# Another order of issue for the pieces of a long-convolution and top-8 expert block

## The chip, the cores and the metric

The kernel runs on one core of one Trainium2 chip. The metric is the device time of one execution in microseconds (us). The engines that compute are TensorE (PE; its weight loads are shown as PEld), VectorE (DVE), ScalarE (ACT) and GpSimd (POOL). SyncE (SP) issues most of the transfers (DMAs); GpSimd and ScalarE issue some. Each engine works through its own queue in the order in which the program issued to it, and waits for others by semaphores.

## The reference, cut to what matters

2048 tokens of width D = 640, bf16. Two residual steps, both with a modulation from one condition vector `c`:

```python
mod = silu(c) @ w_mod                 # 6 rows of 640: sa, ca, ga, sb, cb, gb
h = layernorm(x) * (1 + ca) + sa
kv = short_conv4(k, shift_k) * v      # causal, 4 taps per channel
y = irfft(rfft(pad(kv)) * rfft(pad(ssm_k)))[:2048] + kv * ssm_D
x = x + ga * (h * y)
h = layernorm(x) * (1 + cb) + sb
r = h @ w_r; idx = top 8 tokens of r
y = (silu(h[idx] @ w_gate) * (h[idx] @ w_up)) @ w_down * sigmoid(r[idx])
out = x + gb * (h + scatter_add(y at idx))
```

## The kernel before, in words

The channels are cut into five blocks b = 0 to 4 of 128. For each block the long convolution of 4096 points is done as a two-stage Fourier transform by matmuls, on the kernel rows (`u = 0`, from `gA`) and on the data (`u = 1`, from `xA`). The work is cut into small pieces, each a Python generator step, and a list written out by hand, `ORDER` (lines 35 to 46), says in which order the pieces are issued. `run` (line 886) takes one step of the named task for each entry; `:n` takes n steps, and a star sets `evac.vector`, so that the piece is evacuated from PSUM by VectorE and not by ScalarE (in the C and AT pieces a star means a copy by ScalarE and then a multiply by VectorE, and no star one multiply by VectorE straight from PSUM). The list has 325 steps. Below, BT1.3 means the fourth step (counted from 0) of task BT1, and a position is the place of a step in the list, from 0 to 324. Nothing is reordered later: a piece's instructions go to the end of each engine's queue when it is issued. Buffers come from rings by tag, so an allocation waits until an older tile of its tag is no longer read.

The pieces, with their lines:

- SA to SH, SB, SC, SD, SE, SG, RA, RAT, TAB, WU, TC: constants, sine tables, a warm-up of TensorE (199 to 326). SG loads the diagonal `Dt` (240). IT (328) transposes the tables `FT` into `IT`.
- LG, LK, LXA, LX, LW, LU, WG, WD: loads. LG loads `gA` (140). LK clears 16 columns of `kT` on GpSimd (128) and loads `kT`, `vT` with transposing DMAs (129, 130). LXA loads `xA` from the scratch `kvd` (145). LX loads a quarter of `xq` (643). LW.a loads column block a of `w_mod` into one of two halves of `early` (553), and needs MOD.(a-2) done. LU loads `uA` from the scratch `Ud` (438). WG loads five pieces of the gate weights and five of the up weights (676, 682), WD two pieces of the down weights, issued by ScalarE (688, 690, 691).
- DIAG builds the four diagonal matrices of the short convolution on GpSimd (309); C does the convolution on TensorE, multiplies by `vT` and stores `kvd` (367 to 373).
- G and X: first stage for `gA` (after an addition of `Dt` on GpSimd, for block 0 on VectorE, 353) and `xA`, four pieces each into `A` (346). BG and BX: second stage, four pieces each into `HX` (386 to 390). P: complex product on VectorE, in place (406 to 410). BT: first inverse stage (422, 424), into `U`, stored to `Ud` by GpSimd (428; by SyncE for block 4). AT: last inverse stage with `uA` (457), times `h`; AA adds it into `xq` (468).
- MOD.a: modulation row a (565), evacuated by ScalarE (569, 571); OG, GB and COL combine the rows. Sx: statistics of the first layer norm on VectorE (649), with the power on GpSimd at the end (652). H: `h` in twelve steps (660, 664, 666); `h` lies in the memory of `early`, so H.0 waits for MOD.5.
- R transposes `xq` for the second norm and for r (523, 533), GR forms the squared sums (478). T.0 to T.9: second norm's scale, top 8, the expert, the scatter into the output. BS, BL prepare the base of the output (TensorE with the identity, 498, 499, or VectorE, 493), N normalizes (709, 712), F multiplies, adds and stores the output (720 to 723).

PSUM tiles rotate through four places, so a piece on TensorE also waits for the evacuation of the piece four before it.

Of the kernel before, what the change touches and what calls it, by code (L numbers as in the profile page):

```python
# [32 lines left out]


ORDER = """
SC SA RA WU LG0 SB0 TAB0 SD SG TAB0 SE LG1 LK0 SB1 RA G0 TAB1 G0*:2 G0 DIAG0 G1 SH LX G1* TAB1 LK1 DIAG1 RAT G1*
BG0* C0:2 IT Sx:2 IT* IT Sx LX LXA0 BG0 C1 G1 C1 BG1:2 Sx LG2 LXA1 Sx BG1 RAT BG0* X0:3 X0* Sx:2 BG1 TC BG0
DIAG3 BX0* BX0:2 DIAG2 LK2 X1 Sx P0 X1 LW LX P0 BX0 G2 C2:2 MOD X1 P0 X1* Sx LW Sx G2 LW BT0 G2 BX1* BX1:3 LXA2
P0 G2 MOD LX P1 LK3 Sx BT0 LG3 P1 Sx BT0 Sx BT0 LW Sx X2 Sx X2 MOD X2 BG2 Sx X2 OG Sx C3*:2 BX2 BG2 BT1 BG2 G3
P1 BX2 BG2 G3* MOD G3 BX2 P2 G3 DIAG4 LW BX2 BT1 LXA3 MOD P1 BT1 LW X3 LK4 X3 P2 BT2 MOD X3 LG4 P2:2 BT2 H:4 BT1  # L40
C4* X3 H BG3:2 C4 G4 BX3 LXA4 BX3 G4 LU1 G4 H G4 BG3 H P3 BX3 BG3* LU0 BX3 BT2 P3 X4 H X4 P3 X4 WG X4 H:2 BT2
BG4 WG:2 BG4 BX4* BX4:2 BG4:2 BX4 P3 LU2 P4 BT3 P4 BT3:3 P4 BT4 P4 H COL BT4:3 H GB AT0* COL AT0* LU3 AA0:2
AT1*:2 AA1:2 AT2* LU4 AT2* R0 WG AA2 AT3* R1 R0 GR WG:2 AA2 WG AT3 AA3:2 AT4* WG R1 R2 AT4 AA4 R3 GR AA4 R2 BS*
WD GR R4 BS* R3 BS* GR:2 WD GR R4 BS T BS WG BL N T N:4 N* N BS N:2 F T F N F N:2 F:2 T F:2 N BS WG BL N T N F T
F N F:2 BS F:4 T F T:3
"""


# [908 lines left out]
```

## Time and profile before

| | |
|---|---|
| time, median of 3 runs | 181.32 us (180.77 to 181.73) |
| the profiled execution | 181.52 us, its span 179.7 us |
| busy: PE, DVE, ACT, POOL | 150.0, 145.2, 138.3, 38.4 us |
| TensorE clock granted, mean | 0.899 of full speed |
| moved by DMA | 40.71 MB |

Times in the profile are counted from the first instruction. PE's busy time overlaps from matmul to matmul, since they are pipelined; the next start tells more than an end. In brackets stands how long the engine was idle ahead of an instruction, and who released it; "issue" means that the profile shows nothing that it waited for.

### The profile page before, as it was taken

The page shows a single profiled execution, that of the slowest core. Times are in us where ns is not written, and L with a number is a line of the kernel's source. Part 1 is how long each engine was busy: PE and PEld are TensorE (multiplying, and loading weights), DVE is VectorE, ACT ScalarE, POOL GpSimd, SP SyncE. Part 2 cuts the span into 40 slices and gives each one's busy share as a digit, 9 for nine tenths or more (in the row PEclk, how much of TensorE's full clock was granted, in tenths as well). Part 3 has the DMA queues.
Part 4 walks back from the last instruction along what each step waited for, and adds up shares of the span by engine and source line. Part 5 has one row for each costly group of instructions (what it writes and reads, how often), then busy time and mean ns, then how long its engine had stood idle before and what let it go on. Part 6 is the DMA issues. An engine that isn't in the chain of part 4 may idle for free.

```text
span 179.7 us, 4741 instructions
## 1 busy us (share of the span) xinstructions
PE 150.0 (83%) x1987; PEld 117.8 (66%) x1987; DVE 145.2 (81%) x265; ACT 138.3 (77%) x149; POOL 38.4 (21%) x86
## 2 busy tenths in 40 slices
PE   2879999994999999999999899996699549277850
PEld 0255868861698769886689699896699423137640
DVE  7199997989499938998999999997669537897940
ACT  3979759993499999999989999976849207999500
POOL 8529942000001168210500010200001002200003
PEclk9999999999699999999999999999569957967555
DMA  6799989999799996999939993794993994045640
GB/s 117 89 225 280 253 232 280 159 244 371 225 284 268 295 298 211 283 236 277 313 151 220 295 363 121 205 405 171 303 344 63 336 326 105 21 175 146 218 150 2
DMA packets 71437, 40.71 MB, mean 227 GB/s; under 512 B 45112, under 2 KB 68216, under 8 KB 71416
## 3 DMA queue, kind: packets, MB, share of 16 engines
q1 hardware_dynamic: 66440, 33.99, 73.5%
q0 software_dynamic: 1232, 4.21, 6.3%
q10 hardware_dynamic: 3744, 2.22, 4.3%
q8 instruction: 15, 0.25, 0.6%
q14 instruction: 6, 0.05, 0.1%
HBM read 24.67 MB, written 10.50 MB: 196 GB/s over the span
## 4 chain that ended last, share of the span: by engine, by line
PE 40%; DVE 21%; DMA 18%; POOL 6%; issue 5%; SPq 4%; ACT 4%; POOLq 1%; DVEq 0%; ACTq 0%
DMA kT<-in_A_k_dram 5%; PE ps L457 5%; PE ps L386 4%; DMA early<-in_w_mod_dram 4%; DVE st L649 4%; DMA Dt<-in_A_ssm_D_dram 3%; PE p L367 3%; PE ps L367 3%; SPq L129 3%; PE ps L523 3%; POOL dg L309 3%; DMA uA<-Ud 2%; DVE A L58 2%; PE ps L390 2%; PE ps L388 2%
## 5 line engine op out<-in xcount | busy, mean ns | idle before, releaser
L386 PE MATMUL ps<-A,FT 128*128 128x256 bf16 x132 | 30.2, 273 | 0.0
L60 ACT CAST HX<-ps 128x1024 bf16<-128x1024 f32 x28 | 28.3, 1078 | 2.2 <-PE ps L390 2.2
L390 PE MATMUL ps<-A,FT 128*128 128x128 bf16 x132 | 29.0, 219 | 0.0
L388 PE MATMUL ps<-A,FT 128*128 128x128 bf16 x132 | 28.9, 219 | 0.0
L60 ACT CAST A<-ps 128x1024 bf16<-128x1024 f32 x26 | 26.2, 1051 | 2.5 <-PE ps L346 2.4
L390 PEld LDWEIGHTS <-FT 128*128 128x128 bf16 x160 | 15.6, 98 | 1.8
L428 POOL DMA_DIRECT2D Ud<-U x8 | 4.7, 593 | 54.1 <-ACT U L60 54.1
L388 PEld LDWEIGHTS <-FT 128*128 128x128 bf16 x160 | 15.6, 98 | 0.7 <-issue 0.2
L386 PEld LDWEIGHTS <-FT 128*128 128x128 bf16 x160 | 15.6, 98 | 0.4
L60 ACT CAST U<-ps 128x1024 bf16<-128x1024 f32 x15 | 15.7, 1129 | 0.1
L422 PE MATMUL ps<-IT,HX 128*128 128x256 bf16 x60 | 13.7, 273 | 0.0
L424 PE MATMUL ps<-IT,HX 128*128 128x256 bf16 x60 | 13.7, 273 | 0.0
L649 DVE BATCH_NORM_STATS2 st<-xq 128x6 f32<-128x320 bf16 x32 | 13.3, 478 | 0.0
L367 PEld LDWEIGHTS <-dg 128*128 128x128 bf16 x80 | 7.6, 98 | 8.5 <-issue 0.6
L309 POOL TENSOR_SCALAR dg<-ident,shk_f 128x128 bf16<-128x128 bf16 x16 | 11.7, 748 | 4.2 <-PE ps L367 2.5
L407 DVE TENSOR_TENSOR HX<-HX 128x2048 bf16<-128x2048 bf16 x10 | 12.2, 1225 | 0.3
L60 ACT CAST base<-ps 128x1024 bf16<-128x1024 f32 x7 | 6.8, 1007 | 7.0 <-PE ps L499 7.0
L406 DVE TENSOR_TENSOR T<-HX 128x2048 bf16<-128x2048 bf16 x10 | 12.2, 1217 | 0.0
L457 PEld LDWEIGHTS <-uA 128*128 128x128 bf16 x160 | 10.4, 107 | 2.4 <-DMA uA<-Ud 2.2
L457 PE MATMUL ps<-RAT,uA 128*128 128x128 bf16 x128 | 9.4, 240 | 2.0 <-DMA uA<-Ud 2.0
L565 PE MATMUL ps<-early 128*128 128x320 bf16 x50 | 8.9, 333 | 2.6 <-DMA early<-in_w_mod_dram 2.6
L346 PEld LDWEIGHTS <-gA 128*128 128x128 bf16 x80 | 7.4, 98 | 4.4 <-DVE gA L353 2.0
(257 smaller groups left out, 395.2 us busy)
## 6 DMA issues: line engine op xcount, KB each, us to landing
uA<-Ud SPq DMA_DIRECT2D x10, 512.0 KB, 6.5
early<-in_w_mod_dram SPq DMA_DIRECT2D x6, 800.0 KB, 6.3
Ud<-U POOLq DMA_DIRECT2D x8, 512.0 KB, 5.2
gA<-in_A_ssm_k_dram SPq DMA_DIRECT2D x5, 512.0 KB, 5.0
xq<-in_A_q_dram SPq DMA_DIRECT2D x4, 640.0 KB, 5.7
kvd<-kvT SPq DMA_DIRECT2D x10, 256.0 KB, 3.0
xA<-kvd SPq DMA_DIRECT2D x5, 512.0 KB, 5.4
wg<-in_B_w_gate_dram SPq DMA_DIRECT2D x5, 432.0 KB, 7.2
```

Source lines behind the costliest of these rows:

```text
L60: self.nc.scalar.copy(out=out, in_=in_)
L309: (V if b == 0 else nc.gpsimd).tensor_scalar(out=dg[:, j, :], in0=ident[:], scalar1=shk_f[:, b, j:j + 1], scalar2=None, op0=ALU.mult)
L367: nc.tensor.matmul(ps[:, i, :], lhsT=diags[b][:, j, :], rhs=kT[:, n0 - j:n0 - j + 512], start=(j == 0), stop=(j == 3))
L386: nc.tensor.matmul(ps[:, i], lhsT=FT[:, 0, k2, :], rhs=A[:, 2 * k2:2 * k2 + 2, u, :], start=True, stop=False)
L388: nc.tensor.matmul(ps[:, i, 0, :], lhsT=FT[:, 1, k2, :], rhs=A[:, 2 * k2 + 1, u, :], start=False, stop=False)
L390: nc.tensor.matmul(ps[:, i, 1, :], lhsT=FT[:, 2, k2, :], rhs=A[:, 2 * k2, u, :], start=False, stop=True)
L406: V.tensor_tensor(out=T2[:], in0=X, in1=Hi, op=ALU.mult)
L407: V.tensor_tensor(out=X, in0=X, in1=Hr, op=ALU.mult)
L422: nc.tensor.matmul(ps[:, i, :], lhsT=hx[:, k2, 0, 1, :], rhs=IT[:, k2, 1:3, :].rearrange("p a b -> p (a b)"), start=True, stop=False)
L424: nc.tensor.matmul(ps[:, i, :], lhsT=hx[:, k2, 1, 1, :], rhs=IT[:, k2, 0:2, :].rearrange("p a b -> p (a b)"), start=False, stop=True)
L457: nc.tensor.matmul(o, lhsT=uA[:, bb, cs * P:(cs + 1) * P], rhs=RAT[:, cs, :].rearrange("p (m e) -> p m e", e=8), start=(cs == 0), stop=(cs ...
L649: V.bn_stats(out=st1[:, m, hf, :], in_=xq[:, m, hf * 320:hf * 320 + 320])
```

## The change

`ORDER` is replaced; no other line differs. The same 325 steps are issued, each once. 25 of them change their star.

```diff
@@ -33,16 +33,16 @@
 
 
 ORDER = """
-SC SA RA WU LG0 SB0 TAB0 SD SG TAB0 SE LG1 LK0 SB1 RA G0 TAB1 G0*:2 G0 DIAG0 G1 SH LX G1* TAB1 LK1 DIAG1 RAT G1*
-BG0* C0:2 IT Sx:2 IT* IT Sx LX LXA0 BG0 C1 G1 C1 BG1:2 Sx LG2 LXA1 Sx BG1 RAT BG0* X0:3 X0* Sx:2 BG1 TC BG0
-DIAG3 BX0* BX0:2 DIAG2 LK2 X1 Sx P0 X1 LW LX P0 BX0 G2 C2:2 MOD X1 P0 X1* Sx LW Sx G2 LW BT0 G2 BX1* BX1:3 LXA2
-P0 G2 MOD LX P1 LK3 Sx BT0 LG3 P1 Sx BT0 Sx BT0 LW Sx X2 Sx X2 MOD X2 BG2 Sx X2 OG Sx C3*:2 BX2 BG2 BT1 BG2 G3
-P1 BX2 BG2 G3* MOD G3 BX2 P2 G3 DIAG4 LW BX2 BT1 LXA3 MOD P1 BT1 LW X3 LK4 X3 P2 BT2 MOD X3 LG4 P2:2 BT2 H:4 BT1
-C4* X3 H BG3:2 C4 G4 BX3 LXA4 BX3 G4 LU1 G4 H G4 BG3 H P3 BX3 BG3* LU0 BX3 BT2 P3 X4 H X4 P3 X4 WG X4 H:2 BT2
-BG4 WG:2 BG4 BX4* BX4:2 BG4:2 BX4 P3 LU2 P4 BT3 P4 BT3:3 P4 BT4 P4 H COL BT4:3 H GB AT0* COL AT0* LU3 AA0:2
-AT1*:2 AA1:2 AT2* LU4 AT2* R0 WG AA2 AT3* R1 R0 GR WG:2 AA2 WG AT3 AA3:2 AT4* WG R1 R2 AT4 AA4 R3 GR AA4 R2 BS*
-WD GR R4 BS* R3 BS* GR:2 WD GR R4 BS T BS WG BL N T N:4 N* N BS N:2 F T F N F N:2 F:2 T F:2 N BS WG BL N T N F T
-F N F:2 BS F:4 T F T:3
+LG1 SC SB0 SA SD TAB0 SG SB1 LG0 WU LK0 SE RA:2 TAB0 TAB1 SH RAT G1:2 DIAG0 G0*:2 LX TAB1 DIAG1 G0* IT* LK1 RAT
+C0*:2 LX G0 G1* Sx IT G1* BG0 IT* LXA0 C1:2 BG0 BG1* LG2 LXA1 LK2 LW BG1 Sx BG0 Sx X0 Sx:2 BG1 X0 X0* LX X0 Sx
+BG0 BG1 BX0* BX0 BX0* DIAG2 TC P0 X1 BX0 P0 LW X1 G2 C2 X1 C2 MOD Sx X1 LW Sx LXA2 P0 LX G2 Sx G2 BT0 DIAG3 P0
+BX1* LK3 BX1:2 MOD LG3 G2 BX1 P1:2 BT0 Sx BT0:2 Sx BG2 MOD X2:2 Sx X2 Sx:4 BT1 X2 Sx BG2 LW C3 C3* P1 BX2:2 BG2
+BX2 G3* P2 G3 LW BX2 DIAG4 BG2 P1 OG G3 LXA3 MOD LW P2 G3 MOD BT1:2 P2 X3 BT1 BG3* LK4 X3 P2 LG4 MOD H WG H X3
+BG3 BT2 H X3 H C4*:2 H BX3 WG BX3:3 P3 BT2 H BT2 H BG3 BG3* G4:2 BT2 G4:2 LXA4 X4 P3 LU1 H X4:2 LU0 H X4 BG4:2
+BT3 P3 H BX4* P3 BX4:3 BG4 P4 WG BG4 BT3 P4 BT3 LU2 BT3 P4 WG BT4 P4 H BT4 COL H BT4:2 AT0* AT1 AA0 AT0* LU3 AA1
+AA0 AT2* AT1* AT2* AA1 AA2:2 R0 COL AT3 GB R1 AA3 R0 LU4 WG:2 GR AT3* AA3 AT4* R2 R1 WG AA4 GR AT4 R3 GR AA4 BS*
+R2 R4 WD R3 BS* GR:2 WG BS* WG GR R4 T BL N* BS N:5 T F T N F:2 WG N WD F:2 BS N BS N T N F:2 BS BL T F:2 N F
+N:2 F:2 N F T F N BS F T F T:3
 """
 
 
```

Positions of steps that the text below speaks of, before and after:

| step | before | after | step | before | after |
|---|---|---|---|---|---|
| LG0.0, LG1.0 | 4, 11 | 8, 0 | LK4.0 | 148 | 152 |
| TAB1.0, RAT.0 | 16, 28 | 15, 17 | BT1.3 | 162 | 150 |
| G0.0, G1.0 | 15, 21 | 21, 18 | C4.0, C4.1 | 163, 168 | 166, 167 |
| IT.0, C0.0 | 33, 31 | 27, 30 | G4.0, BX3.3 | 169, 184 | 181, 173 |
| C1.0, C1.1 | 42, 44 | 41, 42 | BT2.3 | 196 | 183 |
| LK2.0, LW.0, LX.2 | 68, 73, 74 | 47, 48, 59 | LXA4.0, X4.0 | 171, 187 | 186, 187 |
| MOD.0, X1.2 | 80, 81 | 79, 77 | WG.0, WG.1 | 192, 198 | 158, 170 |
| Sx.6, Sx.7, Sx.8 | 59, 70, 84 | 80, 83, 88 | WG.3 | 239 | 216 |
| Sx.16, OG.0 | 121, 120 | 120, 138 | BT3.0, BT3.3 | 210, 214 | 198, 214 |
| LW.4, MOD.4 | 139, 143 | 133, 145 | GB.0 | 224 | 241 |
| MOD.3, LW.5, MOD.5 | 133, 146, 152 | 141, 142, 156 | LU3.0, LU4.0 | 228, 236 | 229, 245 |
| H.0 | 158 | 157 | WD.0, R4.0, WD.1 | 263, 265, 271 | 264, 263, 291 |

Stars: to VectorE go G0.0, IT.0, IT.2, G1.3, BG1.0, X0.2, BX0.2, G3.0, BG3.0, N.0; from VectorE go G1.1, BG0.0, IT.1, BG0.2, X0.3, X1.3, G3.1, N.5; a copy by ScalarE is added to C0.0, C0.1, C4.1, AT3.1 and taken from C3.0, AT1.0, AT3.0.

## Rows read from the trace of the kernel before

**Rows 1.** Busy us by stretch: PE, PEld, DVE, ACT, POOL, clock, DMA share, GB/s.
```profile
44.40:117.40 73.00, 72.00 (x704) 59.39 (x705) 65.75 (x99) 68.25 (x76) 15.02 (x17) 0.98 0.95 254
```
**Rows 2.** Timeline of PE around the first modulation product: start, us, engine, line.
```profile
39.92 1.89 PE L367 MATMUL ps<-kT,dg 128*128 128x512 bf16 x8
44.43 2.83 PE L565 MATMUL ps<-early 128*128 128x320 bf16 x10 [2.62 <-DMA early<-in_w_mod_dram]
47.05 1.00 PE L346 MATMUL ps<-RA,xA 128*128 128x256 bf16 x4
47.89 0.60 PE L346 MATMUL p<-RA,xA 128*128 128x256 bf16 x4
```
**Rows 3.** The waits of VectorE: waited for, us in total, times, longest.
```profile
DVE gA L353 <- DMA Dt<-in_A_ssm_D_dram: 3.0, 1, 3.0
...
DVE A L58 <- PE p L346: 2.7, 2, 2.3
```
**Rows 4.** Timeline of SyncE's queue, three issues of loads.
```profile
37.66 0.57 SPq L553 DMA_DIRECT2D early<-in_w_mod_dram  x1
...
73.19 1.15 SPq L553 DMA_DIRECT2D early<-in_w_mod_dram  x1
74.52 5.60 SPq L129 DMA_TRANSPOSE kT<-in_A_k_dram  x1
```
**Rows 5.** Groups by line: an evacuation by VectorE: busy, mean ns.
```profile
L58 DVE CAST HX<-ps 128x1024 bf16<-128x1024 f32 x5 | 6.1, 1216 | 0.2 <-PE ps L390 0.2
```
**Rows 6.** Issue to landing by tile: early (w_mod), kT, xA.
```profile
DMA to landing us min/median/max: 5.1/6.3/9.7
...
DMA to landing us min/median/max: 5.8/7.5/9.9
...
DMA to landing us min/median/max: 4.3/5.4/7.3
```
**Rows 7.** Timeline of POOL: block 1's store, kT4's clear, block 3's store.
```profile
78.76 0.63 POOL L428 DMA_DIRECT2D Ud<-U  x1 [5.70 <-ACT U L60]
79.40 0.13 POOL L128 MEMSET kT<- 128x16 bf16 x1
...
115.21 0.53 POOL L428 DMA_DIRECT2D Ud<-U  x1 [1.29 <-ACT U L60]
```
**Rows 8.** Timeline of SyncE's queue: loads of uA, for block 2, then 3 and 4.
```profile
112.09 1.00 SPq L438 DMA_DIRECT2D uA<-Ud  x2
...
123.15 3.98 SPq L438 DMA_DIRECT2D uA<-Ud  x4
```
**Rows 9.** Timeline of VectorE: P4's last step, AA4's two steps.
```profile
114.94 0.68 DVE L410 TENSOR_TENSOR HX<-HX,T 128x1024 bf16<-128x1024 bf16 x1
...
137.79 1.28 DVE L468 TENSOR_TENSOR xq<-xq,t 128x1024 bf16<-128x1024 bf16 x2
```
**Rows 10.** Timeline of PE: AT3's first matmuls, then R4.0 to GR.4.
```profile
127.27 1.89 PE L457 MATMUL ps<-RAT,uA 128*128 128x128 bf16 x16 [2.04 <-DMA uA<-Ud]
...
139.13 1.01 PE L523 MATMUL ps<-ident,xq 128*128 128x128 bf16 x15
141.25 0.23 PE L523 MATMUL ps<-ident,xq 128*128 128x128 bf16 x1 [1.10 <-issue]
141.31 0.54 PE L533 MATMUL pq<-wcol,xT 128*128 128x3 bf16 x16
141.78 1.07 PE L478 MATMUL pg<-xT 128*32 128x32 bf16 x104
143.22 0.22 PE L478 MATMUL pg<-xT 128*32 128x32 bf16 x7 [0.37 <-ACT xT L527]
146.34 0.31 PE L478 MATMUL pg<-xT 128*32 128x32 bf16 x17 [2.90 <-issue]
```
**Rows 11.** Timeline of VectorE in the last part: T.1's first step, F.0.
```profile
151.56 0.28 DVE L753 CAST T<-pq 16x128 f32<-16x128 bf16 x1 [0.32 <-PE pq L751]
...
154.12 0.82 DVE L720 TENSOR_TENSOR FT<-FT,modv 128x1280 bf16<-128x1280 bf16 x1 [0.59 <-ACT FT L712]
```

## The prediction

> **What bounds the kernel now.** I read the long windows first, then the PE timeline, then the waits, and last each queue beside the two lists of pieces. Between 44.4 and 117.4 us PE is busy for 72.0 of 73.0 us, ACT for 68.3 and DVE for 65.8 [rows 1]: three engines are nearly full at once, so an order can win there only what is idle, a few us. The one large hole ahead of that stretch is the first modulation product: C2's last piece begins at 39.92 and is issued in 1.7 us, then PE stands for 2.62 us until w_mod's first column block lands, and the product runs at the half clock, 2.83 us [rows 2]. VectorE stood for 3.0 us at the start for Dt, and 2.7 us in all for evacuations of A behind that product [rows 3]. The tail is different: a chain of transfers, small VectorE steps and dense small matmuls, with holes of several us [rows 8 to 11]. So I look for the gain in the tail, and for the risk in the full stretch.
>
> **The loads that move but do not.** SyncE issues in list order, and it is compared with itself, not with the pieces between. Taken alone, its order is LG2, LXA1, LK2, LW.0, LX.2 before and after; LW.0 was issued right behind kT2 and vT2, at 37.66 [rows 4]. Moving LW.0 up 25 places and LK2 up 21 therefore moves neither. They still hang on kvd1, that is on C1. I cost them at 0.
>
> **The front (items 0 to 78).** Block 1's gA goes first and the tables of the second half and of RAT are put under the 3.0 us wait for Dt [rows 3]; that is up to 3.0 us of VectorE work hidden. Against it: G1's addition is on GpSimd, gA0's addition now stands behind these tables on VectorE, and IT.0 is issued ahead of C0 and needs the second table's cosines. The best case is 3.0 us earlier, the worst as much later as PE now stands at MOD.0, 2.6 us, without any loss. Since MOD.0 waits for a transfer whose place on SyncE is unchanged, I take 0.
>
> **MOD.0.** One piece, X1.2, passes ahead of it: 0.84 us of PE at the half clock (47.05 to the next piece at 47.89) [rows 2] moves into the hole. Sx.6, Sx.7 and Sx.8 fill VectorE there, in place of most of the 2.7 us it stood for A [rows 3]. I take -0.6; the ends are 0 and -2.2 (the product at the other level as well: 2.83 down to about 1.4).
>
> **The full stretch (items 79 to 224).** Nothing is added, but the marks change: nine evacuations go to VectorE and seven leave it, 1.22 us each [rows 5], so about +2.4 us there; of the C pieces three become a copy on ACT plus a multiply out of SBUF and one goes back, which returns a part. OG's two multiplies pass behind Sx.16. So VectorE has 1 to 2.5 us more to do in this stretch, and it is earlier by the 2 us won at MOD.0. New waits: MOD.3 is 8 places later, so LW.5, which needs its buffer, is issued later than 73.19 [rows 4] while MOD.5 moves 4; MOD.4 on the contrary comes close behind LW.4. With landings of 5.1 to 9.7 us (median 6.3) [rows 6] I get about 1 us of standing at MOD.4. H.0 stands directly behind MOD.5 (h lies in the memory of w_mod's blocks), so what is late there is late for VectorE's twelve H steps. LK4 passes behind BT1.3's store on GpSimd's queue: kT4's clear, at 79.40 now, right behind the store issued at 78.76 [rows 7], comes perhaps 1.7 us later. C4 comes 3 places later, which covers most of it. The G4 pieces behind BX3 cost nothing: A4's buffer is free there, and X4 follows. I take +1.0 for the stretch, from -1.0 (VectorE's 2 us kept) to +4.1 (w_mod at 9.7). P4's end then goes from 115.6 [rows 9] to about 116.0.
>
> **AT, AA, R (items 225 to 263).** Now BT3's second store leaves GpSimd at 115.21 [rows 7], behind U evacuations that ACT does late; it has landed when SyncE starts the next uA load, at 123.15 [rows 8], and AT3's first matmul starts when that is done, at 127.27 [rows 10]. After: BT3.0 moves 12 places up, BT2.3 13, ACT has less to do, gate pieces WG.0, WG.1 and WG.3 go into idle time of the DMA queues, and LU2 (112.09 [rows 8]) no longer shares the queues with BT3's stores. I expect the store 1.5 us earlier, landing 3 us earlier, LU3 at 120 behind U4's second store. Then VectorE sets the pace: from P4.3 I add H.10, H.11, COL, ten multiplies and ten AA pieces, and GB, to AA4.1 between 136 and 137.5, where it ended at 139.07 [rows 9]; counted from P4's end, 0.4 later, that is -2.0 to -3.5. I take -2.2; ends -4.0 and +1.0 (GB and the VectorE multiplies of AT1.0, AT3.0 each one more step ahead of R).
>
> **The instruction waits.** In R4 and GR.4 PE stands 1.10 and 2.90 us for nothing but issue [rows 10]. Between the two lie 1 + 16 + 104 + 7 = 128 matmuls, each with its weight load: PE ran through 256 instructions in 2.2 us and then stood, which looks like a block of instructions fetched too late. Both borders are counted from the end of R4, whose order of matmuls is unchanged, so they stay where they are; but AT4.1, R3.0 and the wait for AA4 now come between the border ahead and R4.0, so the first wait should go (-1.1). The second is 1.8 us longer than the first, and it falls where the blocks of wd and wu are loading; WD.0 now comes behind R4.0 and WD.1 20 places later. I take -0.5 of the 1.8. Together -1.6; ends -2.6 and +1.2. WD.1's new place is harmless: it is issued some 15 us ahead of T.7, and no load in [rows 6] took 10.
>
> **The last part (items 264 to 324).** N.0 goes to VectorE and two identity products pass behind N.1 and N.2, so VectorE does not stand 0.32 us for the transpose and 0.59 us for ScalarE's first N [rows 11]; the rest is the same saturated run of F. I take -0.6 (0 to -0.9).
>
> **Sum.** 0 - 0.6 + 1.0 - 2.2 - 1.6 - 0.6 = -4.0 us. The profiled execution took 181.52 us (span 179.7), 0.2 above the median of 181.32, so 177.5 by its own time, 177.3 beside the median; I give 177.4.
>
> **Rivals.** *The fetch stays* (0.18): the -1.6 is missing, 178.9 to 179.5. For it: the waits are tied to counts that do not move. *The front and MOD.0 win too* (0.12): 175 to 176. For it: VectorE's 3.0 us. *The full stretch eats it* (0.13): MOD.4 or MOD.5 stand for w_mod at its longest, +3.1 over what I took: 180.6; against it stands the median. *Slower* (0.15): block 4 becomes one late chain, kT4, C4, kvd4, xA4, X4, P4, U4, AT4. kT4's clear 1.7 us later, its landing at the median 7.5 in place of the 4.9 us from the clear (79.5) to 84.4 (its 9.9 us are counted from the issue at 74.52 [rows 4, 6]), and xA4 at 7.3 in place of the shortest, 4.3 [rows 6], are 7.3 us; about 1.7 are covered. +5.6: 183.1. It decides when X4's first matmul waits over 4.5 us. For it: C4's multiplies stand behind four H pieces, and two gate loads now pass ahead of xA4 on SyncE; against it: 20 pieces lie between C4 and X4. [...] *Nothing happens*, since SyncE's order hardly changes, lies inside the fourth case.
>
> **Numbers.** Forecast 0.42. A measurement here tells 0.5% (0.9 us) from no change: faster is below 180.4, slower above 182.2. Faster: 0.42 + 0.18 + 0.12 = 0.72; same, most of the full-stretch case, 0.12; slower 0.16 with its worst end. The range runs from the front's case to the slow chain's lower part, 174.6 to 182.8.
>
> **What would show it.** Right: LW.0 issued within 1 us of 37.7; MOD.0's hole under 2.2 us; P4.3 between 115 and 117; LU3 at about 120; R4's first matmul at about 137; no issue wait in R4.0; F's first step at about 150. Wrong: PE standing for kT4, xA4 or w_mod for over 2 us behind 70 us, P4.3 beyond 118, or LU3 still at 123.

## The result, and the profile after

The changed kernel took 176.23 us in the median of 4 runs (174.65 to 177.44), the kernel before 181.05 (180.36 to 181.73) beside it; the ratio is 0.966, interval 0.961 to 0.971. Forecast were 177.4 us and a range of 174.6 to 182.8. On a second chip the changed kernel took 175.97 us (12 runs, 174.51 to 177.69) and the kernel before 179.50 (23 runs; one execution of 297 us apart, 175.84 to 183.91); the ratio there is 0.987, interval 0.981 to 0.993, counted over undisturbed executions alone, of which the kernel before has few, and the ratio of the two medians is 0.980. So the gain is 1 to 4%, and the new order also spreads less.

The profiled execution of the changed kernel took 177.34 us, its span 175.6 (179.7 before). Cut at five marks, in us. P4 ends with its last step on VectorE, GR.4 with its last matmul; the runs e0 to e4 are told of further down:

| profile | P4 ends | to R4.0 | to the end of GR.4 | to F.0 | to the end | span |
|---|---|---|---|---|---|---|
| before | 115.63 | 23.50 | 7.52 | 7.47 | 25.61 | 179.7 |
| before, second profile (e4) | 116.40 | 20.10 | 8.05 | 8.19 | 26.10 | 178.8 |
| after | 118.88 | 19.92 | 4.51 | 6.55 | 25.70 | 175.6 |
| after, second profile (e0) | 118.68 | 19.84 | 4.81 | 6.53 | 25.56 | 175.4 |
| e1: new order to position 224 | 117.34 | 19.12 | 7.18 | 7.40 | 25.57 | 176.6 |
| e2: new order from 225 on | 115.11 | 22.50 | 3.76 | 6.54 | 25.68 | 173.6 |

The first and third rows differ by +3.25, -3.58, -3.01, -0.92 and +0.09, in sum -4.17 us. So in this pair of profiles the change loses 3 us up to P4's end and wins 7.5 behind it. The second profiles of the two kernels differ by +2.28, -0.26, -3.24, -1.66 and -0.54, in sum -3.4: the loss and the gain behind R4.0 are there again, the 3.58 up to R4.0 is not.

**Around MOD.0.** The timeline of PE after, which answers to [rows 2]:

```profile
40.48 1.89 PE L367 MATMUL ps<-kT,dg 128*128 128x512 bf16 x8
44.42 1.53 PE L565 MATMUL ps<-early 128*128 128x320 bf16 x10 [2.05 <-DVE early L560]
45.79 0.60 PE L346 MATMUL p<-RA,xA 128*128 128x256 bf16 x4
```

MOD.0 starts where it started, and the hole is still 2.05 us. But it is now held by VectorE's copy of silu (line 560, begun at 43.55): w_mod's block was issued at 37.35 and landed at 42.35, against 44.30 before. (In the second profile of the kernel before, e4, and in e2, which has its first part, the block landed at 42.78 and 43.57 and the hole is 2.04 and 2.05 us, held by the copy as well: the 2.62 us for the load was that one execution's.) And the product took 1.53 us and not 2.83: TensorE's granted clock stayed at 1.00 of full speed from 42 to 48 us, behind this hole, where before it was 0.50 during the product.

**The full stretch**, by the waits of the changed kernel (waited for, us in total, times, longest), and by the timelines of VectorE, PE, SyncE and GpSimd:

```profile
PE ps L346 <- DVE HX L58: 4.3, 1, 4.3
...
DVE kvT L78 <- DMA vT<-in_A_v_dram: 3.6, 1, 3.6
```
```profile
86.20 1.51 DVE L660 TENSOR_SCALAR h<-xq,rs,nm 128x640 bf16<-128x640 bf16 x4
91.31 1.29 DVE L78 TENSOR_TENSOR kvT<-kvT,vT 128x1024 bf16<-128x1024 bf16 x2 [3.61 <-DMA vT<-in_A_v_dram]
...
97.75 1.51 DVE L660 TENSOR_SCALAR h<-xq,rs,nm 128x640 bf16<-128x640 bf16 x4
99.17 1.22 DVE L58 CAST HX<-ps 128x1024 bf16<-128x1024 f32 x1
```
```profile
100.45 1.01 PE L346 MATMUL ps<-RA,gA 128*128 128x256 bf16 x4 [4.34 <-DVE HX L58]
101.25 1.06 PE L346 MATMUL p<-RA,gA 128*128 128x256 bf16 x4
```
```profile
78.88 3.82 SPq L130 DMA_TRANSPOSE vT<-in_A_v_dram  x1
...
106.82 1.81 SPq L438 DMA_DIRECT2D uA<-Ud  x2
...
122.41 5.35 SPq L438 DMA_DIRECT2D uA<-Ud  x4
```
```profile
80.37 0.55 POOL L428 DMA_DIRECT2D Ud<-U  x1 [2.12 <-ACT U L60]
80.91 0.13 POOL L128 MEMSET kT<- 128x16 bf16 x1
...
115.79 0.54 POOL L428 DMA_DIRECT2D Ud<-U  x1 [17.13 <-ACT U L60]
117.62 0.53 POOL L428 DMA_DIRECT2D Ud<-U  x1 [1.28 <-ACT U L60]
```

The same load and block 1's second store in the kernel before (the store at 85.47 is block 2's first, since BT2.1 stands ahead of BT1.3 in the old list):

```profile
80.21 3.68 SPq L130 DMA_TRANSPOSE vT<-in_A_v_dram  x1
```
```profile
85.47 0.55 POOL L428 DMA_DIRECT2D Ud<-U  x1 [5.94 <-ACT U L60]
86.38 0.53 POOL L428 DMA_DIRECT2D Ud<-U  x1 [0.37 <-ACT U L60]
```

Read them backwards. PE stands 4.34 us ahead of G4.2, for the place in PSUM that BG3.3's evacuation frees. VectorE does that only at 99.17, behind three H steps and P3.0, because it had stood 3.61 us for vT4 at 91.3. And vT4, issued at 78.88, took 12.3 us to land (5.8 before): from 80.37 on, block 1's second store runs beside it and takes 10.6 us itself. Before, that store left at 86.38, when vT4 had landed (86.01), and took 4.6. In all eight profiles in which the two run side by side vT4 lands 0.24 to 0.27 us behind this store. Behind PE's hole TensorE runs at its lower level, 0.50 of full speed from 100 to 104 us, as the windows show.

**The tail.** VectorE at P4's and AA4's last steps and in the last part, and PE at AT3 and from R4.0 on, the answers to [rows 9, 11] and to [rows 10]:

```profile
118.20 0.68 DVE L410 TENSOR_TENSOR HX<-HX,T 128x1024 bf16<-128x1024 bf16 x1
...
138.05 0.69 DVE L468 TENSOR_TENSOR xq<-xq,t 128x1024 bf16<-128x1024 bf16 x1
...
147.96 0.45 DVE L709 TENSOR_SCALAR FT<-xq,sn 128x640 bf16<-128x640 bf16 x1
148.32 0.27 DVE L753 CAST T<-pq 16x128 f32<-16x128 bf16 x1
...
149.86 0.81 DVE L720 TENSOR_TENSOR FT<-FT,modv 128x1280 bf16<-128x1280 bf16 x1
```
```profile
127.12 1.07 PE L523 MATMUL p<-ident,xq 128*128 128x128 bf16 x16 [1.01 <-DVE xq L468]
...
128.46 1.07 PE L457 MATMUL ps<-RAT,uA 128*128 128x128 bf16 x16
...
138.80 1.07 PE L523 MATMUL ps<-ident,xq 128*128 128x128 bf16 x16
139.70 0.54 PE L533 MATMUL pq<-wcol,xT 128*128 128x3 bf16 x16
140.18 1.07 PE L478 MATMUL pg<-xT 128*32 128x32 bf16 x104
141.67 0.22 PE L478 MATMUL pg<-xT 128*32 128x32 bf16 x7 [0.42 <-ACT xT L527]
143.04 0.28 PE L478 MATMUL pg<-xT 128*32 128x32 bf16 x17 [1.15 <-issue]
```

AT3 no longer waits for its transfer (2.04 us in [rows 10]), and PE's longest stop there is 1.0 us for VectorE's addition. LU3 is issued 3.5 us behind P4's end, not 7.5 as before [rows 8, 9] (5.3 in e4): block 3's and 4's four stores took 4.1, 3.5, 3.2 and 3.5 us to land, against 7.2, 7.8, 6.4 and 5.6 (4.5 to 6.2 in e4). LU2, issued at 106.82 and not at 112.09 [rows 8], is out of their way; that this is the reason no run shows by itself. R4.0 runs without the stop of 1.10 us, and GR.4's stop is 1.15 and not 2.90. VectorE starts T.1 without a stop behind N.0, as it should.

### The profile page after: what moved, and what is told of

Same layout as the page of the kernel before. It is cut to its first block, busy times and chain, and to the rows that moved or that the text cites. A ratio compares the mean times of both kernels' runs of the same rounds, so it can differ in the third digit from the quotient of the medians.

```text
span 175.6 us, 4736 instructions
## 1 busy us (share of the span) xinstructions
PE 148.3 (84%) x1987; PEld 116.3 (66%) x1987; DVE 146.7 (84%) x267; ACT 137.0 (78%) x148; POOL 37.2 (21%) x86
## 4 chain that ended last, share of the span: by engine, by line
PE 43%; DVE 31%; DMA 8%; ACT 8%; issue 5%; POOL 1%; POOLq 1%; DVEq 0%; ACTq 0%; SPq 0%
DMA vT<-in_A_v_dram 7%; PE ps L346 5%; PE ps L386 5%; PE ps L367 4%; PE ps L457 3%; PE ps L565 3%; DVE HX L407 3%; DVE T L406 3%; PE ps L390 2%; PE ps L388 2%; PE p L367 2%; DVE IT L722 2%; PE p L346 2%; PE ps L422 2%; PE ps L424 2%
## 5 line engine op out<-in xcount | busy, mean ns | idle before, releaser
L60 ACT CAST HX<-ps 128x1024 bf16<-128x1024 f32 x27 | 27.1, 1043 | 4.0 <-PE ps L390 3.9
L386 PE MATMUL ps<-A,FT 128*128 128x256 bf16 x128 | 29.3, 272 | 0.3 <-ACT HX L60 0.3
L390 PE MATMUL ps<-A,FT 128*128 128x128 bf16 x128 | 28.0, 219 | 0.0
L388 PE MATMUL ps<-A,FT 128*128 128x128 bf16 x128 | 28.0, 219 | 0.0
L60 ACT CAST A<-ps 128x1024 bf16<-128x1024 f32 x23 | 23.2, 1034 | 3.9 <-PE ps L346 3.9
L60 ACT CAST U<-ps 128x1024 bf16<-128x1024 f32 x14 | 14.4, 1061 | 0.2 <-PE ps L424 0.2
L367 PE MATMUL ps<-kT,dg 128*128 128x512 bf16 x56 | 12.9, 379 | 0.0
L422 PE MATMUL ps<-IT,HX 128*128 128x256 bf16 x56 | 12.8, 273 | 0.0
L424 PE MATMUL ps<-IT,HX 128*128 128x256 bf16 x56 | 12.8, 272 | 0.0
L346 PE MATMUL ps<-RA,gA 128*128 128x256 bf16 x60 | 8.8, 282 | 4.3 <-DVE HX L58 4.3
L60 ACT CAST A<-p 128x1024 bf16<-128x1024 f32 x10 | 10.3, 1029 | 0.5 <-PE p L346 0.5
L346 PEld LDWEIGHTS <-xA 128*128 128x128 bf16 x80 | 8.4, 108 | 2.0
```

The source lines that it names most:

```text
L60: self.nc.scalar.copy(out=out, in_=in_)
L346: nc.tensor.matmul(ps[:, bb // 2, :, (bb % 2) * 8:(bb % 2) * 8 + 8], lhsT=src[:, 4 * g4 + bb, :], rhs=RA[:].rearrange("p k c e -> p (k c) ...
L367: nc.tensor.matmul(ps[:, i, :], lhsT=diags[b][:, j, :], rhs=kT[:, n0 - j:n0 - j + 512], start=(j == 0), stop=(j == 3))
L386: nc.tensor.matmul(ps[:, i], lhsT=FT[:, 0, k2, :], rhs=A[:, 2 * k2:2 * k2 + 2, u, :], start=True, stop=False)
L388: nc.tensor.matmul(ps[:, i, 0, :], lhsT=FT[:, 1, k2, :], rhs=A[:, 2 * k2 + 1, u, :], start=False, stop=False)
L390: nc.tensor.matmul(ps[:, i, 1, :], lhsT=FT[:, 2, k2, :], rhs=A[:, 2 * k2, u, :], start=False, stop=True)
```

## The experiments

My theory after this: the tail wins by two things, the stores and the instruction waits; the full stretch loses by one, vT4 against the store. Rivals: one execution showed what others don't; the early gate loads, or the star on BG3.3, make the hole; the tail's gain hangs on the tail's own order.

### e0 and e4: each kernel once more

The edit is none: a second profile of the changed kernel and of the kernel before.

> The changed kernel once more, for a second profile beside the others of this batch. In its first profile vT4 took 12.3 us to land, VectorE stood 3.6 us for it, and PE stood about 4.5 us ahead of G4.2. Theory (the order does it): again vT4 over 9 us, PE idle over 3 us ahead of G4.2, P4's last step at 118 to 120. Rival (that one execution did it): vT4 under 8 us, the hole under 1.5 us, P4's last step at 114 to 116. Time 174.5 to 177.5.

Measured: 175.97 us, vT4 11.4 us, PE idle 3.17 us ahead of G4.2, P4's end at 118.68. It is the order's doing.

> The kernel before once more, for a second profile of it. Theory (the differences between the two traces belong to the order): vT4 lands within 7 us of its issue, P4's last step at 115 to 116, from there 23 to 24 us to R4's first matmul, the stores of block 3's and 4's inverse pieces 5.6 to 7.8 us each, PE's wait for issue in R4.0 about 1 us and in GR.4 2 to 3 us, time 179.5 to 181.5. Rival (some of them are one execution's): P4's last step to R4 under 21 us, or the wait in GR.4 under 1.5 us.

Measured: 178.67 us in the median of 13 runs. vT4 6.2 us, P4's end at 116.40. From PE's timeline and its windows (PE, PEld, DVE, ACT and POOL busy, clock, DMA share, GB/s) of this second profile of before:

```profile
138.59 0.23 PE L523 MATMUL ps<-ident,xq 128*128 128x128 bf16 x1 [1.07 <-issue]
...
144.24 0.32 PE L478 MATMUL pg<-xT 128*32 128x32 bf16 x17 [3.45 <-issue]
```
```profile
124.00:128.00 4.00, 2.79 (x50) 2.62 (x48) 3.91 (x7) 3.98 (x4) 0.00 (x0) 1.00 1.18 314
128.00:132.00 4.00, 3.41 (x130) 3.19 (x128) 3.32 (x6) 2.51 (x3) 0.00 (x0) 1.00 1.16 329
```

The instruction waits are the order's too, 4.52 us in sum. But R4.0 came 20.1 us behind P4's end, not 23.5: the rival holds for this mark. In the first profile the same two windows show the clock at 0.80 and 0.50:

```profile
124.00:128.00 4.00, 1.79 (x24) 1.61 (x24) 3.57 (x6) 4.00 (x5) 0.00 (x0) 0.80 0.89 249
128.00:132.00 4.00, 4.00 (x109) 3.95 (x108) 2.19 (x6) 2.75 (x3) 0.00 (x0) 0.50 1.20 300
```

So the two profiles of the kernel before differ by 3.4 us on this way, and in the longer one TensorE's clock fell to its lower level in PE's stop for AT3 (2.04 us there, 1.21 here): 1.00 from 125 to 126 us, 0.50 from 127 to 133. In the eleven profiles with the new first part it was 1.00 in every window from 117 to 137 us, nearly all of the way from P4's end to R4.0.

### e1 and e2: the new order in halves

Of two lists one half each: e1 issues the 225 steps that the new list has first, in its order, and the other 100 in the old order; e2 the old list's first 225, and the rest in the new order.

> The first 225 pieces of the new order, the rest in the old order. Theory (the full stretch lost 5 us of what the front won, and the gain is the tail's): P4's last step at about 118.9 as in the changed kernel, then the old tail's 64.1 us from there to the end of the span: 184 to 185. Rival (a late P4 costs the old tail less, since that tail stands for its transfers anyway, and the transfers now start with the new part's inverse pieces): 180 to 182.

Measured: 179.89 us (12 runs), ratio to before 1.006, interval 0.996 to 1.016: as the rival has it, a little under its range. vT4 took 10.1 us, P4 ended at 117.34, and R4.0 followed in 19.12 us with block 3's and 4's stores at 3.1 to 4.1 us. The short way from P4 to R4.0 thus belongs to pieces ahead of position 225 (the stores, through BT2.3, BT3 and LU2, by my reading); it is 4.4 or 1.0 us shorter than the old order's 23.50 and 20.10. In time the new first part alone wins nothing. The instruction waits were 1.59 and 2.07 us, the old order's.

> The first 225 pieces of the old order, the rest in the new order. Theory (the tail holds the whole gain; from P4's last step to the end of the span it took 56.7 us after and 64.1 before): P4's last step at 115.6, then 57 to 58: span 173, time 174 to 175. Rival (the inverse pieces, the gate loads and the stores moved ahead of position 225 are what made the tail short): R4's first matmul at 138 to 139 as before, and only the instruction waits and the last part gain, 177.5 to 179.5.

Measured: 176.37 us (6 runs, 174.88 to 180.81), ratio 0.988, interval 0.974 to 1.001, between theory and rival. P4 ended at 115.11; R4.0 took 22.5 us, the clock at 0.79 from 124 to 132 us; then only 3.76 us to GR.4's end with one wait of 0.39, and 6.54 to F.0. These two marks, 10.3 us against 15.0 in the first profile of before, are the tail's own order; the shorter way to R4.0 is not, though in this profile the fall of the clock, behind stops of 1.36 and 0.92 us, is part of it. In time e2 gains what the whole change gains beside the same kernel before, 0.988 against 0.987.

### e3, e5, e6: what makes vT4 late, and what that costs

e3 moves two gate loads back:

```diff
-MOD H WG H X3
+MOD H:2 X3
...
-BX3 WG BX3:3 P3
+BX3:4 P3
...
-H X4 BG4:2
+H X4 WG:2 BG4:2
```

> The changed kernel with the first two gate loads moved back behind X4, where they stood before. Theory (these loads share the transfer engines with kT4, vT4, gA4 and make vT4 late, which makes VectorE late, and so the place in PSUM that G4.2 waits for): vT4 lands within 8 us of its issue, VectorE's wait for it under 0.8 us, the hole ahead of G4.2 under 1.5 us, P4's last step at 115 to 116.5, time 173 to 174. Rival (VectorE's list of evacuations is the cause, not the transfer): vT4 faster, but PE still idle 3 us or more ahead of G4.2, 175.5 to 177.

Measured: 175.51 us; vT4 11.4 us, the hole 3.17 us: the gate loads are not what makes vT4 late, the theory fell. P4 ended at 117.39, 1.3 us earlier than in e0, but behind the same hole the clock stayed up in this execution (1.00 from 100 to 120 us, 0.86 in e0), which can account for this; in time e3 and e0 can't be told apart.

e5 takes the store off GpSimd's queue:

```diff
+                if kk == 1 and b == 1 and hk == 1:
+                    late[1] = U
-                if kk == 1:
+                elif kk == 1:
...
+    def t_ST():
+        nc.sync.dma_start(out=Uds[1][:, 8:16, :], in_=late[1][:])
+        yield
...
-G4:2 LXA4 X4
+G4:2 ST LXA4 X4
```

> The changed kernel, but block 1's second store (issued by GpSimd at 80.4 us while vT4 is loading) is issued by SyncE ahead of xA4's load, some 13 us later. Theory (BT1.3 moved ahead of the key load makes this store run against vT4's transposing load; each slows the other): vT4 within 8 us of its issue instead of 11.4 to 12.3, VectorE's wait for it under 1 us instead of 2.8 to 3.6, PE's hole ahead of G4.2 under 2 us instead of 3.2 to 4.3, P4's last step 1.5 to 3 us earlier, time 173 to 174.5. Rival (gA4 and kT4 make vT4 late, or VectorE's marks the hole): vT4 still over 10 us or the hole still over 3 us, time 175 to 177.

Measured: 174.81 us (6 runs), ratio to before 0.973, interval 0.965 to 0.981. SyncE's queue and PE in this run:

```profile
80.21 3.28 SPq L130 DMA_TRANSPOSE vT<-in_A_v_dram  x1
...
91.45 0.40 SPq L436 DMA_DIRECT2D Ud<-U  x1
92.94 0.37 SPq L145 DMA_DIRECT2D xA<-kvd  x1
```
```profile
98.31 0.60 PE L346 MATMUL ps<-RA,gA 128*128 128x256 bf16 x4 [0.51 <-DVE HX L58]
98.75 0.60 PE L346 MATMUL p<-RA,gA 128*128 128x256 bf16 x4
101.18 1.48 PE L346 MATMUL ps<-RA,xA 128*128 128x256 bf16 x12 [1.83 <-DMA xA<-kvd]
```

vT4 took 5.7 us, VectorE did not stand for it, and the hole at G4.2 is 0.51 us. So the store was the cause of vT4's delay. It now meets xA4, which took 8.2 us, and X4 stands 1.83. P4 ended at 116.82, 1.9 earlier than in e0, although PE's G2.3 came at 53.65 in this execution and not at 51.98, as where TensorE's clock falls at MOD.0 (in e6 it was 0.50 from 46 to 48 us).

e6 takes the star from BG3's last piece (`BG3 BG3*` becomes `BG3:2`):

> The changed kernel with one star taken away: BG3's last evacuation goes to ScalarE. Theory (PE's hole ahead of G4.2 stands for this evacuation alone, which VectorE reaches only behind P3.0 and two H steps): the hole under 1 us instead of 3.2 to 4.3, P4's last step 1.5 to 3 us earlier, time 173 to 174.5. Rival (VectorE is late as such, by vT4, and what comes next waits for it instead: X4 for kvd4, or BX4 for PSUM): the hole moves on by a few pieces, P4's last step within 1 us of 118.7, time 175 to 176.5.

Measured: 176.03 us; the hole at G4.2 is gone, and this stands in its place:

```profile
97.48 0.60 PE L346 MATMUL ps<-RA,gA 128*128 128x256 bf16 x4
98.15 0.60 PE L346 MATMUL p<-RA,gA 128*128 128x256 bf16 x4
101.61 1.48 PE L346 MATMUL ps<-RA,xA 128*128 128x256 bf16 x12 [2.87 <-DMA xA<-kvd]
```

With vT4 at 11.2 us C4's product, kvd4 and xA4 are late, and X4 waits 2.87 us: the time is the rival's, and the wait moved as it said, though P4's end (117.37) came 1.3 us earlier than in e0, more than it said. BG3.3's star was only where the late vT4 was felt first.

### e7 and e8: the instruction waits

e7 takes the last two WG pieces, which load up weights, from ahead of GR.4 (`GR:2 WG BS* WG GR R4` becomes `GR:2 BS* GR R4 WG:2`):

> The changed kernel with its last two gate loads moved from ahead of GR.4 to behind R4.1, so that none of their transfers runs while PE passes GR.4. Theory (PE's wait for issue there is a fetch of instructions that shares the transfer engines with the loads: 2.9 us before, with two loads running, 1.2 to 1.4 us after): the wait 0.6 us or less, R4.1 0.7 us or more earlier, time 175 to 175.5 beside the changed kernel's 176.0, if the up weights do not come late. Rival (it has a fixed length, or hangs on what PE did ahead of it): the wait still 1.1 to 1.5 us, time 175.7 to 176.5. Second rival: the last piece of the up weights lands after the gate products and the expert waits: 177 or more.

Measured: 176.36 us, the wait 1.76 us, above both guesses. It tells nothing for or against: SyncE does not wait for PE, and the transfers ran as before, another piece at 140.28 to 146.65 among them.

e8 makes them wait: the second of the up pieces is issued by ScalarE behind BL's evacuation, and the two after it, and the first half of the down weights, stand behind it in the list.

```diff
-            nc.sync.dma_start(out=w_sb[:, :, f0:f1], in_=up[:, :, f0:f1])
+            eng = nc.scalar if f0 == 1035 else nc.sync
+            eng.dma_start(out=w_sb[:, :, f0:f1], in_=up[:, :, f0:f1])
...
-R4 T BL N* BS
+R4 T BL WG:3 WD N* BS
```

> The changed kernel with the last three middle pieces of the up weights and the first half of the down weights held back: the first of them is issued by ScalarE behind BL's evacuation, which waits for PE's work behind GR.4, and the others hang on it, so that no weight load runs while PE goes from R4.0 to GR.4. In the profiles so far the packet of the instruction queue moved 0.15 to 3.0 us after PE had begun a block of 256 instructions, and the next block began 2.2 to 2.9 us after the packet. Theory (the packet waits behind the loads): packet within 0.4 us of R4.0's end, PE's wait for issue in GR.4 0.7 us or less instead of 1.2 to 1.8. Rival (the packet's delay is fixed, or hangs on something else): packet again about 1 us late, wait 1.1 us or more. The time itself may rise, since the weights come 5 us later: 175 to 178.

Measured: 177.75 us, 1.8 above e9 of the same batch; the profile does not show that the late weights cost this, for from P4's end to the end of the span it took 56.85 us, and 56.74 in e0. PE's timeline, and the DMAs from 139 to 144 us (packets; by queue: packets, MB, share of 16 engines):

```profile
143.83 0.28 PE L478 MATMUL pg<-xT 128*32 128x32 bf16 x17 [1.22 <-issue]
```
```profile
DMA packets 1, 0.02 MB, mean 3 GB/s; under 512 B 0, under 2 KB 0, under 8 KB 0
## 3 DMA queue, kind: packets, MB, share of 16 engines
q8 instruction: 1, 0.02, 1.2%
```

In five microseconds nothing moved but one packet of instructions, and the wait was still 1.22 us: the rival. The packets show more. I take the last matmul of R4.0 as the beginning of a block and the stop in GR.4 as the beginning of the next, and find each packet in windows of 0.2 us:

| profile | packet ahead | block begins | packet | next block begins | packet to packet |
|---|---|---|---|---|---|
| before | 138.4 | 141.25 | 143.8 | 146.34 | 5.4 |
| e4, before | 135.8 | 138.59 | 141.6 | 144.24 | 5.8 |
| e1, old tail | 136.6 | 139.06 | 140.8 | 143.34 | 4.2 |
| after | 136.8 | 139.65 | 140.6 | 143.04 | 3.8 |
| e0, after | 136.8 | 139.37 | 140.8 | 143.03 | 4.0 |
| e2, new tail | 135.2 | 138.46 | 138.6 | 141.10 | 3.4 |
| e8, queues empty | 137.8 | 140.37 | 141.4 | 143.83 | 3.6 |

In all seven PE goes on 2.2 to 2.6 us behind the packet (2.7 in e7), and in none do two packets lie under 3.4 us apart, empty queues (3.6 in e8) or not. PE works through this block in about 2.1 us (140.37 to 142.44 in e8), so by my reading it runs out of instructions here and stops. How long it stops seems to hang also on how late PE comes to the block: in e2, with the same tail, it began 3.3 us behind the packet ahead, against 2.6 to 2.9 in after, e0 and e8, and stopped for 0.39 us only. Above the 3.4 to 4.0 us of the new tails stand the old ones, 4.2 to 5.8, where w_down's and w_up's loads run (344 GB/s from 141 to 147 us before, 143 from 139 to 143 after). That these loads make the difference was not shown by a run of its own: e7 failed to move them, and e8 took away loads from an order that hardly suffered from them. The page of the profile counts 15 such packets of 0.25 MB in all. If all of them are PE's, its 1987 matmuls and as many weight loads make 265 instructions each, an estimate, where I had counted 256 between the stops.

### e9, e10, e11: undoing the losses

e9 ends the first step of `t_MOD` behind line 560 (a `yield`), and issues it ten pieces earlier (`DIAG2 TC P0` becomes `DIAG2 TC MOD P0`):

> The changed kernel with the silu of the condition vector and its copy on VectorE issued some ten pieces earlier, ahead of C2 and of P0.0. In the changed kernel MOD.0 stood 2.0 us for this copy, since w_mod's block had landed at 42.4 while the copy began at 43.55. Theory (the copy is the last thing MOD.0 waits for): MOD.0 begins at 42.4 to 42.8, PE idle ahead of it under 0.5 us, TensorE's clock stays at its upper level there in every execution, P4's last step 1 to 2 us earlier, time 174 to 175. Rival (the 2 us are lost again in the full stretch, where vT4 and the store set the pace): P4's last step within 0.7 us of 118.8, time 175.5 to 176.3.

Measured: 175.95 us. PE's timeline:

```profile
51.94 0.60 PE L346 MATMUL p<-RA,gA 128*128 128x256 bf16 x4 [1.42 <-DVE HX L58]
```

MOD.0 began at 42.81, without a hole and at the upper clock (its product took 1.52 us, as against 2.83 at 0.50 before), 1.6 us earlier; at G2.3 (which the expectation of e11 calls G2's first piece) all of it was gone, 51.94 against 51.98, in a stop for VectorE's evacuation. P4 ended at 119.56. By the time the rival holds (P4's end lies just outside its 0.7 us), but the gain is lost long before vT4: VectorE sets the pace there.

e10 is e5 with the store behind xA4 and LU0 on SyncE:

```diff
-ST LXA4 X4 P3 LU1 H X4:2 LU0 H X4
+LXA4 LU0 ST X4 P3 H X4:2 LU1 H X4
```

> As the run with block 1's second store moved to SyncE, but now behind xA4's load and the first of LU0's, with LU1 behind it, so that the store meets neither vT4 nor xA4's beginning. In that run vT4 took 5.7 us, and PE then stood 1.8 us for xA4, which took 8.2. Theory (the store slows whichever load it meets): vT4 under 7 us, xA4 under 6 us, no hole over 1 us at G4.2 or X4.0, P4's last step at 114.5 to 116.5, time 172.5 to 174. Rival (xA4 is slowed by the loads of uA or by gate loads and not by the store): xA4 over 7 us again, 174.5 to 175.5. Second rival: LU1 waits for the store and holds SyncE, gate pieces and LU2 come late, and the tail loses it: 175 to 177.

Measured: 174.35 us (6 runs, 173.22 to 174.91), ratio to before 0.982, interval 0.973 to 0.990; e9, in the same batch on the same chip, took 175.95, as the changed kernel did on another chip (175.97). vT4 took 5.7 us, xA4 4.4, between 92 us and P4's end PE has no hole over 0.6 us, and P4 ended at 114.66, 4.0 us earlier than in e0. So the store slowed vT4 in one place and xA4 in the other, and neither here. Not every load beside a store is slowed: before, vT4 took 5.8 us beside block 1's first store (78.76 to 84.12). LU1 went out only at 102.65, and R4.0 came 20.48 us behind P4's end, 0.6 more than in e0.

e11 is e9 and e10 together:

> The last two edits together: the silu copy early, and block 1's second store on SyncE behind xA4 and LU0. With the silu early alone MOD.0 began 1.6 us sooner, but the first piece of G2 at 51.94 us began as in the changed kernel (51.98), behind 1.42 us of standing for VectorE. Theory (VectorE sets the pace there, so the silu is worth nothing also where the store no longer makes vT4 late): the hole of 1.4 us at 51.9 again, P4's last step at 114 to 115.2 as with the store alone (114.66), time 173.8 to 174.8 beside the 174.35 of the store alone. Rival (the 1.6 us was lost only to vT4's wait and comes through now): P4's last step at 113 to 113.6, time 172 to 173.3.

Measured: 173.82 us (6 runs, 173.65 to 174.51), ratio 0.979, interval 0.972 to 0.986. MOD.0 at 42.81, then 51.94 with 1.42 us of standing again, P4's end at 115.11: the theory. It is the fastest here and spreads least; it beats the kernel before, beside which it ran, and lies 2.1 to 2.4 us under the changed kernel, which did not run on this chip. By its six runs it can't be told from e10.

## Why the prediction was right

The time was right to 1.2 us (177.4 against 176.23), and every part's sign behind P4 was right. But up to P4's end the first two profiles differ by 2.9 us more than forecast and behind it by 3.0 us less, so the closeness of the sum is luck. By its steps:

- **Loads that move but do not: right.** LW.0 was issued at 37.35, within 1 us of 37.7.
- **The front, 0: right** within its bounds. VectorE's 3.0 us for Dt [rows 3] are gone (GpSimd waits 1.6 for it now), and still C2's last piece begins at 40.48, 0.6 later than in [rows 2].
- **MOD.0, -0.6: a wrong holder, and a size that doesn't count.** The hole was under 2.2 us as named, but the copy of silu held it, not the load, as it does in two of three profiles with the old first part; the clock stayed up (1.00), so that PE was 2.1 us ahead behind it, the far end. By e9 and e11 earlier work on PE here is given back to VectorE by 52 us. That the stretch behind it takes the gain away, I had allowed only as "VectorE has 1 to 2.5 us more to do".
- **The full stretch, +1.0: the step that failed.** P4 ended at 118.88, where 115 to 117 was right and beyond 118 wrong: 2.9 us later than the 116.0 I gave, and 5.3 later than PE's lead of 2.1 would give. The term's own parts were misread: of the nine and seven evacuations only two and two lie in items 79 to 224 (G3.0, BG3.0; X1.3, G3.1), and one C piece each way. VectorE's busy time from 44.43 to P4's end did rise, from 64.0 to 66.2 us, but by Sx.6 and Sx.7, which moved behind MOD.0 (1.9 us): the amount was right by luck. And MOD.4 does not come closer behind LW.4: it stands 12 places behind it, where it stood 4. I had the place, BT1.3 ahead of LK4, and looked at the wrong effect: the clear of kT4 behind the store on GpSimd's queue, 1.7 us (it came 1.5 later). What counts is that the store's transfer runs against vT4's, 12.3 us for 5.8 (e5, e10). The waits for w_mod that I feared did not come. The slower rival's chain came in part, through vT4 and not kT4 or xA4; X4 never waited its 4.5 us in the changed kernel, since G4.2 stood first, and e6 shows X4 waiting 2.87 where it doesn't.
- **The gate loads against xA4: no effect seen.** Moving them away left xA4 at 5.0 us, against 5.3 and 4.6 with them, and vT4 as late, 11.4 us (e3). Transfers that different engines issued did come in each other's way in another place: block 1's second store on GpSimd's queue and vT4 on SyncE's took 10.6 and 12.3 us where they meet and 4.6 and 5.8 where they don't.
- **AT, AA, R, -2.2: right mechanism, unsteady size.** The stores take 2 to 4 us less to land, LU3 follows P4's end 4.0 us sooner (1.7 by the second profile of before), and VectorE sets the pace. By the clock on paper LU3 came at 122.41 and R4.0 at 138.80, not 120 and 137, as P4 was late. From P4's end it is -3.6 against the first profile of before and -0.2 against the second; between those two lies a fall of the clock (0.50 from 128 to 132 us in the first, 1.00 in the second), which no profile with the new first part shows there and for which the sum has no term.
- **The instruction waits, -1.6: right, undersized.** The first went, as forecast; the second fell from 2.90 to 1.15 us where I took 0.5 off. In sum -2.85 (and a new stop of 0.26 in GR.1). What is left stays even with empty queues (e8): that the packets keep a distance, 3.6 us even there, was not in my term.
- **The last part, -0.6: right**, -0.92, at its far end; F.0 at 149.86.

## What to carry to other kernels

When a store is moved past a load in the list, look at what its transfer then runs beside, not only at what stands behind it in its engine's queue: here one 512 KB store doubled a transposing load's time (12.3 us for 5.8), and moving it away gave 1.6 us (e10 against e9, on one chip; e9's own edit gave nothing). Where several engines are nearly full, test what a closed hole gains at the next meeting point: here the 1.6 us won at MOD.0 were gone at G2.3, 9 us later, in 1.42 us of standing for VectorE (e9, e11). Where PE runs dense small matmuls and stands for nothing but issue, count the instructions from stop to stop. Here they were 256, worked through in about 2.1 us, with packets 3.4 us or more apart, and PE stood for 0.39 to 3.45 us in GR.4. In the new order the first stop, 1.10 us before, was gone; that a wait which PE has anyway does this where it falls between two stops was my reasoning, and no run shows it.

## What the runs showed that I had not expected

Packets of instructions followed each other by 3.4 us or more, by 3.6 with every other queue empty (e8), and where PE stopped for one it went on 2.2 to 2.9 us behind it; what sets this distance stays open. And of nine profiles with the same hole of 2 us ahead of MOD.0 (all with the new front but e9 and e11) TensorE's clock stayed up in five (1.00 in after), and fell in four (e1, e5, e6, e8; 0.50 from 46 to 48 us in e6), where G2.3 then came at 53.65 to 53.72 and not at 51.98; what decides between the two was not tried. Nor was it tried why vT4, and not every load beside a store, is held until the store has landed.
